# A decode block on one core: the last head's w_o rows four at a time, an empty pass skipped, the last V piece cut 10 + 6, and smaller edits to the layer norms and the gate product

## The chip, the cores and the metric

One Trainium2 chip, one core of it in use. The metric is the device time of one execution in microseconds (us), as a median over several executions. The engines named below are PE (TensorE: PE for its matmuls, PEld for its weight loads), DVE (VectorE), ACT (ScalarE), POOL (GpSimd) and SP (SyncE, which here only issues DMAs).

## The reference

One token (x is 1 x 512) goes through an attention block with a cached K and V, and then through a gated feed-forward block. All arrays are bfloat16.

```
h  = x + attention(layernorm(x))     # 32 query heads on 8 K/V heads; 65536 cached keys of 128 numbers each
     q = layernorm(x) @ wq           # 512 x 4096
     o = softmax(q k^T / sqrt(128)) v
     ... o @ wo                      # 4096 x 512
h2 = h + (sigmoid(n @ w_gate) * (n @ w_up)) @ w_down,   n = layernorm(h)   # 512 x 1792, 1792 x 512
```

K and V are 128 MB each; wq and wo 4 MB each; the three feed-forward weights 1.75 MB each. Each byte is read once, and the result is 1 KB.

## The kernel before

**Loads.** Every input but x goes through the one DMA queue of SP, in the order in which the program lists the loads (L332 to L361). K and V arrive in halves of a head (8 MB, `load`, L324) in a ring buffer in SBUF. A load waits for a mark that says that its place in the ring is free. For the last head the order in SP's queue is: the first half of V7 (L344); w_o in two pieces (L345 to L348, `WO`: the 28 rows per partition of heads 0 to 6, then the 4 of head 7), the first of which waits until PE is through with V6; the second half of V7 in two pieces (L349, `LAST`: 12 chunks of 512 KB, then 4); w_gate, w_up and w_down (L351 to L361), which wait until PE is through with the first half of V7. `WD_SPLIT` (L236) cuts w_down's 14 rows per partition into 8, 4 and 2.

**Attention.** DVE transposes K chunks (L517), PE computes scores of four blocks per head (`pe_scores`), ACT takes the exponentials, DVE transposes the probabilities, and PE multiplies them with V (`pv`, L591): a round is 8 matmuls, two chunks of V by four column groups of 32 of the PE array, the results in partitions 0, 32, 64 and 96 up. A half of V is 8 rounds: 6, a check, and 2. PE's program for all heads is one hand-written loop (`pe_flow`, L673) with a head as the outer step and four parts as the inner one. Register `w` counts the parts, `i` the heads, `m` and `k` the rounds. The V rounds of head h-1 run in parts 1 and 3 of head h. A ninth pass has no scores left and only does the V rounds of head 7: its parts 0 and 2 are empty, and PE goes through their branches and register instructions only. In its part 3, ahead of the second half of V7, stands section L (`project7`, L640): `regroup(0)` puts the outputs of heads 0 to 6 into 28 columns (L620 to L629), `rows` multiplies each of these columns (as 128 x 1 weights) with 512 columns of w_o, two matmuls to a pass of a loop, all into one row of PSUM (L645 to L663), DVE copies this row (L665), and `columns` turns it into four columns with float32 matmuls (L671). Section VL (L795) waits for the last piece of V7 ahead of the last two rounds.

**The tail.** `head_out` (L603) brings out head 7, `regroup(1)` and `project` (L631) add its 4 rows of w_o, which gives h as four columns of 128. `ln_stats` (L385) takes h, its square and their sums (four DVE instructions), and a matmul with ones adds over the partitions (L391). `hc` (L808) is h less its mean; the reciprocal deviation (`ln_rstd`, L394, with a power on POOL) is applied later, at the activation. 32 matmuls compute gate and up (L821), ACT takes the tanh that stands for the sigmoid (L828), DVE multiplies it with up (L831) and transposes the product (L834), 56 matmuls with one weight column each multiply it with w_down (L839, rows r = 0 to 13 by column groups g = 0 to 3), on top of h, which a matmul with `gsel` has put into the same four PSUM rows (L826). Two copies on DVE and two on ACT bring these rows into one row in SBUF (L845, L847), and one DMA from SP writes the 1 KB (L849). The program ends when that DMA has landed.

The layer norm of x at the start uses the same `ln_stats`; its result is needed by the query projection (L463), which also needs wq.

Of the kernel before, what the change touches and what calls it, by code (L numbers as in the profile page):

```python
# [6 lines left out]
bf16 = mybir.dt.bfloat16  # L7
# [8 lines left out]
NQ = 32  # L16
DH = 128
D = 512
# [197 lines left out]
def bass_sequential_preLN__gqa_block_cached__glu_gated_glu__decode_kernel(  # L216
# [19 lines left out]
    WD_SPLIT = [(0, 8), (8, 12), (12, 14)]  # L236
    FG = FF // 4

    with ExitStack() as es:
# [22 lines left out]
        yr = sb("yr", [1, 512], fp32)  # L262
        po_sb = sb("po_sb", [128, 512], bf16)
        one_f = sb("one_f", [1, 1], fp32)
        zcol = sb("zcol", [128, 1], bf16)
        XR = 16
# [27 lines left out]
        hhT = sb("hhT", [128, FG], bf16)  # L294
        y_sb = sb("y_sb", [1, D], bf16)
# [23 lines left out]
        LAST = [(16, 28), (28, 32)]  # L319
# [25 lines left out]
        for i, (j0, nj) in enumerate(WO):  # L345
            src = A_wo[j0 * DH:(j0 + nj) * DH, :].rearrange("(p r) n -> p (r n)", r=nj)
            dst = ktw[:, j0 * D:(j0 + nj) * D]
            dma("sp", lambda e, src=src, dst=dst: e.dma_start(dst, src), f"wo{i}", [f"PV{h - 1}.3"] if i == 0 else (), f"wo{i}")  # L348
        for i, cols in enumerate(LAST):  # L349
            load("V", h, 1, (), ("vb", "vl")[i], f"V{h}.1{('', 'b')[i]}", cols)  # L350
        for k, w in (("wg", B_w_gate), ("wu", B_w_up)):  # L351
            src = w.rearrange("(p k) n -> p (k n)", p=128)
            for i, (k0, k1) in enumerate(W_SPLIT[k]):
                at = W_AT[k]
                dma("sp", lambda e, at=at, w=src, a=k0 * FF, z=k1 * FF: e.dma_start(ring[:, at + a:at + z], w[:, a:z]),
                    f"{k}{i}", [f"PV{HKV - 1}.1"] if k == "wg" else (), f"{k}.{i}")
# [8 lines left out]
        for nm, t, v in (("onesf", onesf[:, :], 1.0), ("xz0", xz[:, :], 0.0), ("onef", one_f[:, :], 1.0), ("nhalf", nhalf[:, :], -0.5),  # L365
                         ("gs0", gsel[:, :], 0.0), ("zcol", zcol[:, :], 0.0), ("qh0", qh[:, :], 0.0), ("qz0", qz[:, :], 0.0),
                         ("PTz", PT_sb[:, 4 * 512:PT_ROW], 0.0), ("Wz", ktw[:, W0:KTW_ROW], 0.0)):
            op("pool", lambda e, t=t, v=v: e.memset(t, v), name=nm)
# [11 lines left out]
        op("dve", lambda e: e.tensor_reduce(bass.AP(tensor=gsel, offset=0, ap=[[128, 128], [32, 4]]),  # L380
                                            identf[:, :].rearrange("p (s j) -> p s j", s=4), AX.X, ALU.add), ["gs0", "identf"], "gsel")
# [3 lines left out]
        def ln_stats(i, fill, dep, bank, c0):  # L385

            op("dve", fill, [dep], f"hT.{i}")
            op("dve", lambda e: e.tensor_tensor(sq[:, :], hT[i][:, :], hT[i][:, :], ALU.mult), [f"hT.{i}"], f"sq.{i}")
            op("dve", lambda e: e.tensor_reduce(st[i][:, 0:1], hT[i][:, :], AX.X, ALU.add), (), f"sta.{i}")
            op("dve", lambda e: e.tensor_reduce(st[i][:, 1:2], sq[:, :], AX.X, ALU.add), [f"sq.{i}"], f"st.{i}")  # L390
            op("pe", lambda e: e.matmul(ps(bank, c0, c0 + 2), lhsT=onesf[:, :], rhs=st[i][:, :], start=True, stop=True),  # L391
               [f"st.{i}", f"sta.{i}", "onesf"], f"tot.{i}")
# [23 lines left out]
        ln_stats(0, lambda e: e.tensor_copy(hT[0][:, :], x_col[:, :]), "xcol", 0, 0)  # L416
# [54 lines left out]
        op("pe", project_q, ["zq", "xz", "wq", "identf", "lsel", "onef", "sel", "gsel", "row", "PTz", "qz0"], "q")  # L471
# [119 lines left out]
        def pv(h, r, rounds):  # L591
            P.part["pe"] = ("B", (h, r, rounds))
            name = f"PV{h}.{r}" + "a" * (rounds == 6)
# [46 lines left out]
        def project7():  # L640
            regroup(0)
            waits = ["O3.0", "wo0"]
            def rows(e):
                out = ps(YB, 0, D, 0, 1)
                e.matmul(out, lhsT=O3[:, 0:1], rhs=ktw[:, 0:D], start=True, stop=False, skip_group_check=True)  # L645
                ra, ro, rb, rp, left = (reg(e, i) for i in range(16, 21))
                n = NQ - GS
                e.reg_mov(ra, addr_of(ktw, D))
                e.reg_mov(ro, addr_of(O3, 1))
                e.reg_mov(left, n // 2 - 1)  # L650
                e.reg_alu(rb, ra, 2 * D, ALU.add)
                e.reg_alu(rp, ro, 2, ALU.add)
# [3 lines left out]
                for x in (ra, rb):  # L656
                    e.reg_alu(x, x, 4 * D, ALU.add)
                for x in (ro, rp):
                    e.reg_alu(x, x, 4, ALU.add)
# [3 lines left out]
                return e.matmul(out, lhsT=O3[:, n - 1:n], rhs=ktw[:, (n - 1) * D:n * D], start=False, stop=True, skip_group_check=True)  # L663
            op("pe", rows, waits, "yr")
            op("dve", lambda e: e.tensor_copy(yr[:, :], ps(YB, 0, D, 0, 1)), ["yr"], "yrs")  # L665

        def columns():

            for nt in range(4):
                lhsT = bass.AP(tensor=yr, offset=nt, ap=[[D, 1], [4, 128]])  # L670
                op("pe", lambda e, lhsT=lhsT, nt=nt: e.matmul(ps(YT, nt, nt + 1), lhsT=lhsT, rhs=one_f[0:1, 0:1], start=(nt == 0),  # L671
                                                              stop=False, skip_group_check=True), ["yrs"] if nt == 0 else ())
        def pe_flow(e, section):  # L673
# [7 lines left out]
            i, w, p, v, m, k, s = (R.setdefault(n, e.alloc_register(f"r_{n}")) for n in "iwpvmks")  # L681
# [8 lines left out]
            e.reg_mov(s, step[0])  # L690
            goto("head")
# [25 lines left out]
            away("br_eq", i, i_last, "rows_of_o", lambda: section("L"))  # L717
# [28 lines left out]
            e.reg_alu(w, w, -4, ALU.add)  # L746
            e.br_ne(w, w0 - 16, on_true="part", on_false="head_end")
            label("head_end")
            e.br_eq(i, i_last, on_true="after", on_false="more_heads")
            label("more_heads")  # L750
            section("X")
            e.reg_alu(i, i, -lag, ALU.add)
            nc.br("head", engines=here)
            for name, body, back, under in later:
                label(name, under)
                body()
                nc.br(back, engines=here)
            label("after", "head_end")
# [11 lines left out]
        for i in range(HKV + 1):  # L770
            loop, last = 0 < i < HKV, i == HKV
            for r in range(NR):
# [12 lines left out]
                if i and r == 3:  # L785
# [6 lines left out]
                    pv(i - 1, r, 6)  # L792
# [3 lines left out]
                    pv(i - 1, r, 2)  # L796
# [10 lines left out]
        ln_stats(1, lambda e: e.tensor_tensor(hT[1][:, :], ps(YT, 0, 4), x_col[:, :], ALU.add), "yT", STB, 0)  # L807
# [23 lines left out]
        op("dve", lambda e: e.tensor_tensor(hh[:, :].rearrange("p (r q) -> p r q", r=NF),  # L831
                                            ps(UB, 0, FG).rearrange("p (q r) -> p r q", r=NF),
                                            sg2[:, :].rearrange("p (q r) -> p r q", r=NF), ALU.mult), ["gu1", "sg2"], "hh")
        op("dve", lambda e: e.transpose(hhT[:, :], hh[:, :]), ["hh"], "hhT")  # L834
        for i, (r0, r1) in enumerate(WD_SPLIT):
            for r in range(r0, r1):
                for g in range(4):
                    last = r == NF - 1 and g == 3
                    op("pe", lambda e, r=r, g=g: e.matmul(  # L839
                        ps(YB, 0, 128, 32 * g, 32 * g + 1), lhsT=hhT[:, 32 * r:32 * r + 1], rhs=wd_v[:, r, g * 128:(g + 1) * 128],  # L840
                        start=False, stop=(r == NF - 1), tile_position=(0, 32 * g), skip_group_check=True),
                       ["hhT", f"wd{i}"] if r == r0 and g == 0 else (), "y" if last else None)
        for g in (0, 2, 1, 3):
            if g < 2:
                op("dve", lambda e, g=g: e.tensor_copy(y_sb[:, 128 * g:128 * g + 128], ps(YB, 0, 128, 32 * g, 32 * g + 1)), ["y"], f"ysb{g}")  # L845
            else:
                op("act", lambda e, g=g: e.activation(y_sb[:, 128 * g:128 * g + 128], ps(YB, 0, 128, 32 * g, 32 * g + 1), AF.Copy),  # L847
                   ["y"], f"ysb{g}")
        dma("sp", lambda e: e.dma_start(out[0], y_sb[:, :]), "out", [f"ysb{g}" for g in range(4)], "out")  # L849
        P.at_end = ("out",)  # L850
# [29 lines left out]
```

## Time and profile before

| | us |
|---|---|
| median of 3 runs | 658.86 (657.86 to 659.07) |
| the profiled execution | 658.92 |
| its span, first to last instruction | 657.6 |
| DMA: bytes read, mean rate over the span | 282.33 MB, 429 GB/s |
| PE busy | 403.7 (61%) |
| DVE busy | 350.7 (53%) |
| ACT busy | 42.9 (7%) |
| mean granted PE clock | 0.78 |

The profiled execution's own time is 1.3 us more than its span; the durations below come from this one execution. "Busy" counts work instructions only, not register, branch, semaphore and DMA-issuing ones. "Landing" of a DMA is counted from the start of its issue on the queue's engine. A row of the timeline gives the start, the time, the engine, the line, the operation, and in brackets the idle time before it with what ended it.

### The profile page before, as it was taken

To read this page: it belongs to the slowest core of one execution; us is meant where nothing else is said; L and a number is where in the kernel's file an instruction comes from. 1 tells how busy PE (TensorE), PEld (TensorE's weight loads), DVE (VectorE), ACT (ScalarE), POOL (GpSimd) and SP (SyncE) were. 2 spreads that over 40 slices of the span, in tenths; PEclk is the share of its full clock that TensorE was granted. 3 is DMA by queue.
4 is the path that set the end of the run, shared out by engine and by line. 5 is a ranking of instruction groups with operands and counts; after the bars stand their busy time and mean duration, and the time that the engine had idled before them with its cause. 6 is when DMAs were issued, how large, how long until landed. Compare 5 with 4: busy or idle time off the path is not lost. (4 is left out here: it accounts for less than half of the span.)

```text
span 657.6 us, 6197 instructions
## 1 busy us (share of the span) xinstructions
PE 403.7 (61%) x2316; PEld 68.8 (10%) x1548; DVE 350.7 (53%) x427; ACT 42.9 (7%) x114; POOL 3.6 (1%) x17
## 2 busy tenths in 40 slices
PE   2688672938547293764829476382946738285585
PEld 0100010110101010010100101010010101001132
DVE  3398853809266390936628183572908457193102
ACT  1100200020000200001000200002000020002001
POOL 1000000000000000000000000000000000000000
PEclk9889796867959587795958769595786959687677
DMA  9999999999999999999999999999999999999996
GB/s 399 431 440 452 442 419 415 446 446 442 431 403 446 446 446 435 395 446 446 446 435 399 442 446 446 442 407 427 446 446 442 419 415 446 446 442 431 419 410 291
DMA packets 6370, 282.33 MB, mean 429 GB/s; under 512 B 737, under 2 KB 738, under 8 KB 1250
## 3 DMA queue, kind: packets, MB, share of 16 engines
q1 hardware_dynamic: 6338, 282.33, 99.3%
q10 hardware_dynamic: 32, 0.00, 0.0%
HBM read 282.33 MB, written 0.00 MB: 429 GB/s over the span
## 5 line engine op out<-in xcount | busy, mean ns | idle before, releaser
L517 DVE STREAM_TRANSPOSE ktw<-ring 128x1024 f32<-128x1024 f32 x256 | 291.7, 1209 | 165.1 <-DMA ring<-in_A_k_cache_dram 165.1
L430 PE MATMUL PS<-ktw 128*128 128x512 bf16 x1024 | 277.8, 421 | 161.3 <-DVE ktw L517 157.5
L430 PE MATMUL PS<-ring,PT_sb 128*32 x1024 | 87.0, 430 | 51.4 <-issue 47.3
L430 PEld LDWEIGHTS PS<-ktw 128*128 x256 | 26.4, 103 | 401.3 <-issue 236.2
L604 ACT ACTIVATE po_sb<-PS,rl 128x512 bf16<-128x512 f32 x8 | 5.5, 687 | 525.0 <-PE PS L430 525.0
L430 PEld LDWEIGHTS PS<-ring,PT_sb 128*32 x1024 | 20.7, 116 | 115.2 <-issue 113.9
L552 DVE TENSOR_REDUCE gmj<-PS 1x4 f32<-1x128 f32 x8 | 2.2, 278 | 54.5 <-PE PS L550 54.5
L524 DVE TENSOR_REDUCE M_sb<-PS 128x1 f32<-128x512 f32 x32 | 19.9, 682 | 19.3 <-PE PS L430 19.3
L563 ACT ACTIVATE P_sb<-PS,negmax 128x512 bf16<-128x512 f32 x32 | 21.6, 686 | 0.3
L573 DVE STREAM_TRANSPOSE PT_sb<-P_sb 128x512 bf16<-128x512 bf16 x32 | 19.9, 675 | 1.7 <-ACT P_sb L563 1.7
L430 PE MATMUL PS<-ktw,xz 128*8 x32 | 8.8, 443 | 3.6 <-DMA ktw<-in_A_wq_dram 3.6
L620 DVE TENSOR_TENSOR Lw<-O,blk_of 128x896 bf16<-128x896 bf16 (+1 forms) x2 | 1.4, 682 | 13.0 <-ACT O L610 13.0
L550 PE MATMUL PS<-identf,gm 128*1 128x128 f32 x16 | 4.5, 380 | 5.5 <-issue 3.4
L629 DVE CAST O<-PS 128x28 bf16<-128x28 f32 (+1 forms) x2 | 0.3, 173 | 14.0 <-PE PS L626 14.0
L557 PE MATMUL PS<-one_f,gmrep 1*128 1x1 f32 x16 | 4.4, 344 | 5.0 <-DVE gmrep L554 5.0
L430 PE MATMUL PS<-ktw,O 128*1 x26 | 7.0, 433 | 0.0
L475 DVE STREAM_TRANSPOSE qt<-qh 32x512 bf16<-32x512 bf16 x1 | 0.7, 699 | 11.5 <-ACT qh L472 11.5
L563 ACT ACTIVATION_READ_ACCUMULATOR P_sb<-PS,negmax 128x1 f32 x32 | 6.5, 203 | 0.0
L607 PE MATMUL PS<-sel_bf,po_sb 128*128 128x4 bf16 x32 | 2.1, 171 | 6.3 <-ACT po_sb L604 6.3
L490 ACT ACTIVATE PS<-zcol 128x512 f32<-128x512 bf16 x8 | 5.0, 621 | 0.0
L559 ACT ACTIVATE negmax<-PS 128x1 f32<-128x1 f32 x8 | 1.4, 172 | 55.1 <-PE PS L557 55.1
L411 PE MATMUL PS<-xs,xpick 16*128 16x32 bf16 x1 | 0.2, 204 | 7.7 <-DMA xs<-in_A_x_dram 7.7
(88 smaller groups left out, 70.0 us busy)
## 6 DMA issues: line engine op xcount, KB each, us to landing
ring<-in_A_k_cache_dram SPq DMA_DIRECT2D x4, 4096.0 KB, 35.3
ring<-in_A_v_cache_dram SPq DMA_DIRECT2D x1, 6144.0 KB, 32.9
ktw<-in_A_wq_dram SPq DMA_DIRECT2D x1, 4096.0 KB, 12.5
ktw<-in_A_wo_dram SPq DMA_DIRECT2D x1, 3584.0 KB, 18.0
ring<-in_A_v_cache_dram SPq DMA_DIRECT2D x1, 2048.0 KB, 37.3
ring<-in_B_w_gate_dram SPq DMA_DIRECT2D x1, 1792.0 KB, 23.3
ring<-in_B_w_up_dram SPq DMA_DIRECT2D x1, 1344.0 KB, 26.0
ring<-in_B_w_down_dram SPq DMA_DIRECT2D x1, 1024.0 KB, 28.7
```

The source lines that it names most:

```text
L430: return e.add_instruction(mybir.InstMatmult(name=nc.get_next_instruction_name(), engine=mybir.EngineType.PE, ins=[rhs, lhsT], outs=[e.low ...
L490: op("act", lambda e: e.activation(ps(PO, 0, 512), bass.AP(tensor=zcol, offset=0, ap=[[1, 128], [0, 512]]), AF.Copy), ["zcol"] if h == 0 e ...
L517: op("dve", lambda e, d=dst, sr=src: e.transpose(d, sr), deps, f"T{b}.{c}", to="T")
L524: op("dve", lambda e, u=u: e.tensor_reduce(M_sb[:, u % 4:u % 4 + 1], ps(u % NS, 0, 512), AX.X, ALU.max), [f"S{b}.{NC - NR + k}"], f"mx{u}" ...
L550: op("pe", lambda e: e.matmul(ps(MISC, 0, 128, 0, 1), lhsT=gm[:, :], rhs=identf[:, :], start=True, stop=True), [f"gm{h}"], f"gmT{h}", to="Q")
L552: op("dve", lambda e: e.tensor_reduce(gmj[:, :], ps(MISC, 0, 128, 0, 1).rearrange("p (i a c) -> p a i c", a=4, c=NC), AX.XY, ALU.max), [f" ...
L557: op("pe", lambda e: e.matmul(ps(MISC, 128, 129), lhsT=gmrep[0:1, :], rhs=one_f[0:1, 0:1], start=True, stop=True), [f"gmrep{h}"], f"neg{h}")
L559: op("act", lambda e: e.activation(negmax[:, k:k + 1], ps(MISC, 128, 129), AF.Copy, scale=-att_scale), [f"neg{h}"], f"negmax{h}")
L563: op("act", lambda e, b=b: e.activation(P_sb[:, (b % 4) * 512:(b % 4 + 1) * 512], ps(b % NS, 0, 512), AF.Exp, bias=negmax[:, k:k + 1], sca ...
L573: op("dve", lambda e, b=b: e.transpose(PT_sb[:, (b % 4) * 512:(b % 4 + 1) * 512], P_sb[:, (b % 4) * 512:(b % 4 + 1) * 512]), [f"E{b}"], f" ...
L604: op("act", lambda e: e.activation(po_sb[:, :], ps(PO, 0, 512), AF.Copy, scale=rl[:, :]), [f"PV{h}.{NR - 1}", f"rl{h}"], f"po{h}", to="po")
L607: op("pe", lambda e, t=t: e.matmul(ps(OX, 0, 4), lhsT=po_sb[:, t * 128:(t + 1) * 128], rhs=sel_bf[:, 8 * t:8 * t + 8:2], start=(t == 0), s ...
```

## The change

- `LAST` cuts the second half of V7 into 10 + 6 chunks, and PE does 5 rounds, the check, and 3. The second piece of w_o (4 rows, 512 KB) is issued behind the V pieces and not ahead of them.
- The ninth pass enters the loop at part 1 and steps by 8 to part 3, so that its empty parts 0 and 2 are not gone through; register `d` holds the step. The loop's way out now stands behind section O of that pass.
- `rows` does four w_o rows to a pass of its loop, one in each column group, into PSUM rows 0, 32, 64, 96 of a bank that ACT clears early (`zy`). So all 128 partitions are copied (L665), and `columns` adds the four by weights of 128 x 128 and a selecting column.
- `ln_stats` takes two DVE instructions that multiply or add two operands and sum the result.
- The gate product and its transpose come in two parts (rows 0 to 6, 7 to 13). `WD_SPLIT` is 9, 4, 1.
- The result's even column groups use 32 weight columns, of which the last is the real one, so that groups 0 and 1 end in the neighbouring partitions 31 and 32, and 2 and 3 in 95 and 96. One copy on DVE and one on ACT, of 33 partitions each, and two DMAs of 2 x 256 B, one issued by SP and one by ACT, take the place of four copies and one DMA.

```diff
-    WD_SPLIT = [(0, 8), (8, 12), (12, 14)]
+    WD_SPLIT = [(0, 9), (9, 13), (13, 14)]
-        LAST = [(16, 28), (28, 32)]
+        LAST = [(16, 26), (26, 32)]
...
+        load_wo(0, [f"PV{h - 1}.3"])
         for i, cols in enumerate(LAST):
             load("V", h, 1, (), ("vb", "vl")[i], f"V{h}.1{('', 'b')[i]}", cols)
+        load_wo(1, ())
...
-            op("dve", fill, [dep], f"hT.{i}")
-            op("dve", lambda e: e.tensor_tensor(sq[:, :], hT[i][:, :], hT[i][:, :], ALU.mult), [f"hT.{i}"], f"sq.{i}")
-            op("dve", lambda e: e.tensor_reduce(st[i][:, 0:1], hT[i][:, :], AX.X, ALU.add), (), f"sta.{i}")
-            op("dve", lambda e: e.tensor_reduce(st[i][:, 1:2], sq[:, :], AX.X, ALU.add), [f"sq.{i}"], f"st.{i}")
+            op("dve", lambda e: e.tensor_tensor_reduce(hT[i][:, :], parts[0], parts[1], 1.0, 0.0, ALU.add, ALU.add, st[i][:, 0:1]), [dep], f"hT.{i}")
+            op("dve", lambda e: e.tensor_tensor_reduce(sq[:, :], hT[i][:, :], hT[i][:, :], 1.0, 0.0, ALU.mult, ALU.add, st[i][:, 1:2]),
+               [f"hT.{i}"], f"st.{i}")
...
+        op("act", lambda e: e.activation(ps(5, 0, 512), bass.AP(tensor=zcol, offset=0, ap=[[1, 128], [0, 512]]), AF.Copy), (), "zy")
...
-                for x, y in ((ra, ro), (rb, rp)):
-                    mm_at(e, out, at_reg(O3, y, [[NQ, 128], [1, 1]]), at_reg(ktw, x, [[KTW_ROW, 128], [1, D]]), False, 32)
+                for g in range(4):
+                    mm_at(e, ps(YB, 0, D, 32 * g, 32 * g + 1), at_reg(O3, ys_[g], [[NQ, 128], [1, 1]]),
+                          at_reg(ktw, xs_[g], [[KTW_ROW, 128], [1, D]]), False, 32, 32 * g)
...
-            op("dve", lambda e: e.tensor_copy(yr[:, :], ps(YB, 0, D, 0, 1)), ["yr"], "yrs")
+            op("dve", lambda e: e.tensor_copy(yr[:, :], ps(YB, 0, D)), ["yr"], "yrs")
-                lhsT = bass.AP(tensor=yr, offset=nt, ap=[[D, 1], [4, 128]])
+                lhsT = bass.AP(tensor=yr, offset=nt, ap=[[D, 128], [4, 128]])
...
-            e.reg_alu(w, w, -4, ALU.add)
+            e.reg_alu(w, w, d, ALU.add)
             e.br_ne(w, w0 - 16, on_true="part", on_false="head_end")
             label("head_end")
-            e.br_eq(i, i_last, on_true="after", on_false="more_heads")
-            label("more_heads")
             section("X")
             e.reg_alu(i, i, -lag, ALU.add)
-            nc.br("head", engines=here)
+            e.br_ne(i, i_last, on_true="head", on_false="last_head")
+            label("last_head")
+            e.reg_mov(w, w0 - 4)
+            e.reg_mov(p, p0)
+            e.reg_mov(d, -8)
+            nc.br("values", engines=here)
...
-                    pv(i - 1, r, 6)
+                    pv(i - 1, r, 5 if last else 6)
...
-                    pv(i - 1, r, 2)
+                    pv(i - 1, r, 3 if last else 2)
...
+        HH = ((0, 7), (7, NF))
+        for i, (r0, r1) in enumerate(HH):
+            op("dve", lambda e, r0=r0, r1=r1: e.tensor_tensor(
+                hh[:, 32 * r0:32 * r1].rearrange("p (r q) -> p r q", q=32),
+                ps(UB, 0, FG).rearrange("p (q r) -> p r q", r=NF)[:, r0:r1, :],
+                sg2[:, :].rearrange("p (q r) -> p r q", r=NF)[:, r0:r1, :], ALU.mult), ["gu1", "sg2"], f"hh{i}")
+            op("dve", lambda e, r0=r0, r1=r1: e.transpose(hhT[:, 32 + 32 * r0:32 + 32 * r1], hh[:, 32 * r0:32 * r1]), [f"hh{i}"], f"hhT{i}")
...
+                    m, c = (1, 32 * r + 32) if g % 2 else (32, 32 * r + 1)
...
+        op("dve", lambda e: e.tensor_copy(y_sb[0:33, :], ps(YB, 0, 128, 0, 33)), ["y"], "ysb0")
+        op("act", lambda e: e.activation(y_sb[64:97, :], ps(YB, 0, 128, 64, 97), AF.Copy), ["y"], "ysb1")
+        for i, eng in enumerate(("sp", "act")):
+            dst = out[0][:, 256 * i:256 * i + 256].rearrange("o (s j) -> (o s) j", s=2)
+            dma(eng, lambda e, i=i, dst=dst: e.dma_start(dst, y_sb[64 * i + 31:64 * i + 33, :]), f"out{i}", [f"ysb{i}"], f"out{i}")
+        P.at_end = ("out0", "out1")
```

Left out: a zeroed column `zf` for the first layer norm, a zeroed start of `hhT`, `gsel` with its ones at columns 31, 32, 95 and 96, a matmul with zeros that closes `rows`, and the wait of the query projection for `zy`.

More of the change, by code (lines that the diff above doesn't have):

```diff
@@ L293, in bass_sequential_preLN__gqa_block_cached__glu_gated_glu__decode_kernel @@
         hh = sb("hh", [128, FG], bf16)
-        hhT = sb("hhT", [128, FG], bf16)
-        y_sb = sb("y_sb", [1, D], bf16)
+        hhT = sb("hhT", [128, 32 + FG], bf16)
+        y_sb = sb("y_sb", [128, 128], bf16)
         W0 = NKT * CH
@@ L592, in pv @@
             P.part["pe"] = ("B", (h, r, rounds))
-            name = f"PV{h}.{r}" + "a" * (rounds == 6)
+            name = f"PV{h}.{r}" + "a" * (rounds > 3)
             for k in range(2):
@@ L643, in rows @@
             def rows(e):
[L644 to L646 removed]
                 n = NQ - GS
[L648 to L652, printed above, removed]
[L653 to L659 removed]
+                xs_, ys_, left = [reg(e, 16 + g) for g in range(4)], [reg(e, 20 + g) for g in range(4)], reg(e, 24)
+                e.reg_mov(xs_[0], addr_of(ktw))
+                e.reg_mov(ys_[0], addr_of(O3))
+                e.reg_mov(left, n // 4)
+                for g in range(1, 4):
+                    e.reg_alu(xs_[g], xs_[0], 2 * D * g, ALU.add)
+                    e.reg_alu(ys_[g], ys_[0], 2 * g, ALU.add)
+                goto("rows")
+                for g in range(4):
+                    mm_at(e, ps(YB, 0, D, 32 * g, 32 * g + 1), at_reg(O3, ys_[g], [[NQ, 128], [1, 1]]),
+                          at_reg(ktw, xs_[g], [[KTW_ROW, 128], [1, D]]), False, 32, 32 * g)
+                for g in range(4):
+                    e.reg_alu(xs_[g], xs_[g], 2 * 4 * D, ALU.add)
+                    e.reg_alu(ys_[g], ys_[g], 2 * 4, ALU.add)
                 e.reg_alu(left, left, -1, ALU.add)
@@ L756, in pe_flow @@
                 body()
-                nc.br(back, engines=here)
-            label("after", "head_end")
+                if name == "outs":
+                    e.br_ne(i, i_last, on_true=back, on_false="after")
+                else:
+                    nc.br(back, engines=here)
+            label("after", "outs")
         def dve_flow(e, section):
@@ L838, in bass_sequential_preLN__gqa_block_cached__glu_gated_glu__decode_kernel @@
                     last = r == NF - 1 and g == 3
-                    op("pe", lambda e, r=r, g=g: e.matmul(
-                        ps(YB, 0, 128, 32 * g, 32 * g + 1), lhsT=hhT[:, 32 * r:32 * r + 1], rhs=wd_v[:, r, g * 128:(g + 1) * 128],
+                    m, c = (1, 32 * r + 32) if g % 2 else (32, 32 * r + 1)
+                    op("pe", lambda e, r=r, g=g, m=m, c=c: e.matmul(
+                        ps(YB, 0, 128, 32 * g, 32 * g + m), lhsT=hhT[:, c:c + m], rhs=wd_v[:, r, g * 128:(g + 1) * 128],
                         start=False, stop=(r == NF - 1), tile_position=(0, 32 * g), skip_group_check=True),
[L842 to L850, printed above, removed]
+                       ((["hhTz", f"wd{i}"] if r == r0 else []) + [f"hhT{j}" for j, (h0, _) in enumerate(HH) if r == h0]) if g == 0 else (), "y" if last else None)
+        op("dve", lambda e: e.tensor_copy(y_sb[0:33, :], ps(YB, 0, 128, 0, 33)), ["y"], "ysb0")
[4 more added lines that the diff above has]
+        P.at_end = ("out0", "out1")
         P.emit()
```

42 lines of the change are left out of this document (23 added, 19 removed).

## The prediction

> **What bounds the kernel now.** I read the page's load lines first: is the stream of loads ever interrupted?
>
> ```profile
> span 657.6 us, 6197 instructions
> ...
> DMA  9999999999999999999999999999999999999996
> ```
>
> All 40 slices but the last are full, so nothing in the middle of the kernel can shorten it: every byte has to come in, and the time is the end of the stream plus what follows it. So the question is where the stream ends. The start of each issue is in the views by line and in the timeline, the time to landing in the DMA view:
>
> ```profile
> L348 SPq DMA_DIRECT2D ktw<-in_A_wo_dram x2: 328/380/433, 602.0 to 602.3; - x2
> 602.82 0.91 SPq L330 DMA_DIRECT2D ring<-in_A_v_cache_dram  x2
> L355 SPq DMA_DIRECT2D ring<-in_B_w_up_dram x2: 432/434/435, 622.0 to 622.5; - x2
> L360 SPq DMA_DIRECT2D ring<-in_B_w_down_dram x3: 432/432/432, 623.0 to 623.9; - x3
> ```
>
> ```profile
> ktw<-in_A_wo_dram SPq DMA_DIRECT2D x1, 3584.0 KB, 18.0
> ktw<-in_A_wo_dram SPq DMA_DIRECT2D x1, 512.0 KB, 18.9
> ring<-in_A_v_cache_dram SPq DMA_DIRECT2D x1, 6144.0 KB, 32.9
> ring<-in_A_v_cache_dram SPq DMA_DIRECT2D x1, 2048.0 KB, 37.3
> ring<-in_B_w_up_dram SPq DMA_DIRECT2D x1, 448.0 KB, 26.7
> ring<-in_B_w_down_dram SPq DMA_DIRECT2D x1, 1024.0 KB, 28.7
> ring<-in_B_w_down_dram SPq DMA_DIRECT2D x1, 512.0 KB, 29.5
> ring<-in_B_w_down_dram SPq DMA_DIRECT2D x1, 256.0 KB, 29.6
> ```
>
> Start plus time (of a merged pair, the second starts half its time later: V's at 603.3): w_o lands at 620.0 and 621.2, the last V half at 635.7 (12 chunks) and 640.6, the last of w_up at 649.2, w_down at 651.7, 652.9 and **653.5**. The 6144 KB took 635.7 - 621.2 = 14.5 us, 424 KB per us; 37.3 - 18.9 us and the others give the same pace, so these loads run one behind the other.
>
> The span goes on for 4.1 us after the last landing. What fills it is in the chain of waits (start, us, what):
>
> ```profile
> 635.83 0.46 issue
> 636.29 5.58 PE PS L430 x42
> 641.87 1.33 issue
> 643.21 0.63 PE PS L430 x8
> ...
> 644.91 0.70 ACT po_sb L604
> ...
> 647.76 0.17 DVE hT L807
> ...
> 648.37 0.60 PE PS L391 x2
> ...
> 648.99 0.17 DVE hc L808
> ...
> 649.21 3.19 PE PS L821 x18
> ...
> 652.42 0.93 DVE hh L831
> ...
> 653.37 0.66 DVE hhT L834
> ...
> 654.07 1.69 PE PS L839 x56
> ...
> 656.09 0.28 DVE y_sb L845
> ```
>
> It begins when the 12 chunks of V land (635.7), and from there never waits for a load again: the other V chunks (640.6) and all weights are in before they are asked for, and the last matmuls start 0.5 us after the last landing, because of `hhT`. So **today compute from V7 on sets the end, with the stream of loads only half a microsecond behind.** A shorter chain can win that half microsecond; what more there is lies in the matmuls that stand behind the last landing, and in the output.
>
> **The change: loads.** The bytes stay. With w_o's 512 KB behind V and 10 chunks (5120 KB), the first V piece lands at 620.0 + 5120/424 = 632.1, the second (3072 KB) at 639.4, w_o's rest at 640.6 as V's end did. w_gate, w_up and w_down keep their places. w_down as 9 + 4 + 1: from 649.2, the first 1024 KB took 2.5, so 1152 KB 2.8: 652.0; then as before 1.2 (512 KB): 653.2; then 128 KB, half of 0.6: 653.5. The last piece comes in 1 KB runs, shorter than any weight run of before; the pace of 2 KB runs (256 KB in 0.6) is that of the long ones, so I count nothing; twice the price would be 0.3 us, which the range takes in. SP issues as many loads as before, and V's are no longer behind one of w_o's.
>
> **PE up to V7.** These rows carry it:
>
> ```profile
> 624.06 0.45 PEld L626 LDWEIGHTS PS<-row_of,Lw 128*128 128x128 bf16 x7 [3.24 <-issue]
> 625.26 6.97 PE L430 MATMUL PS<-ktw,O 128*1 x26
> 632.49 0.68 DVE L665 COPY yr<-PS 1x512 f32<-1x512 f32 x1 [7.66 <-PE PS L663]
> 633.22 2.02 PE L671 MATMUL PS<-one_f,yr 1*128 1x1 f32 x8 [0.77 <-DVE yr L665]
> 636.28 0.16 PEld L430 LDWEIGHTS PS<-ring,PT_sb 128*32 x8 [1.13 <-issue]
> 641.23 0.16 PEld L430 LDWEIGHTS PS<-ring,PT_sb 128*32 x8 [0.81 <-issue]
> ```
>
> Between V7's first half and the weights of 624.06 PE idles through part 2's empty pass and part 3's branches; halving that saves about 1.2. Of the 28 w_o rows 26 take 6.97, so all take 7.5. Four at a time are what a V round does twice; a round takes (641.23 - 636.28)/5 = 0.99, so seven passes take 3.5: 4 us less. The copy (L665) and `columns` (L671) now work on 128 partitions, which isn't in the trace: from below as long as before (0.7 + 2.0), from above twice that. I take the first, since the columns are as many. So PE is ready for V7 near 630.0 instead of 635.2 (633.22 + 2.02). **All that is worth nothing by itself**: it is covered by the wait for V, which ends at 632.1; at twice the price PE is ready at 632.7, which costs 0.6 of the 1.8 us that it then waits for the next piece. But without it V would start 3 us late: old `columns` ended only 0.5 before the old landing.
>
> V resumes at 632.1 + 0.5 = 632.6; 5 rounds end near 637.6, and **a new wait** of 1.8 us comes, for the 6 chunks at 639.4. Behind it on PE stand the last rounds and everything after; the feed-forward weights do not wait for it. It resumes after 0.5 (as after 635.83) to 1.3 us (the gap at 641.87); I take 0.6: 640.0. Three rounds: 2.0 to the last one's start, and 0.63 to 1.0 for it by the clock: 642.7 to 643.0, against 644.9. So the chain is about 2 us earlier at po_sb.
>
> **The tail's small edits.**
>
> ```profile
> L430 PE MATMUL PS<-ktw,xz 128*8 x32 | 8.8, 443 | 3.6 <-DMA ktw<-in_A_wq_dram 3.6
> L388 DVE TENSOR_TENSOR sq<-hT 128x4 f32<-128x4 f32 x1 | 0.2, 163 | 0.0
> L563 ACT ACTIVATION_READ_ACCUMULATOR P_sb<-PS,negmax 128x1 f32 x4 | 0.8, 203 | 0.0
> L839 PEld LDWEIGHTS PS<-ring,hhT 128*1 128x1 bf16 x56 | 1.4, 120 | 1.3 <-DVE hhT L834 1.3
> L810 DVE TENSOR_TENSOR hz<-sel_f,hT 128x128 f32<-128x128 f32 x1 | 0.3, 281 | 0.0
> ```
>
> Layer norm: from 647.76 to the matmul at 648.37 is 0.61. Two dependent instructions of 0.2 (163 ns plus a gap) make 0.45: 0.15 less. An instruction with a sum isn't in the trace; if the sum is read out separately as on ACT (203 ns each), it is 0.25 more. I take -0.15, being nearest to L388. For x it hardly matters: the query matmuls wait for wq (the first row). Extra clears (POOL, 0.1 each; ACT 0.6) lie in the first 5 us, where both idle later.
>
> From po_sb to hc were 648.99 - 644.91 = 4.1, from hc to the end of gate and up 3.4. So hc comes at 646.6 to 647.2 (the upper with short matmuls at half clock), the others end at 650.0 to 650.6 (w_up's last piece, 649.2, is in before its turn). Gate product: two halves of 0.54 (of 0.92, 0.16 fixed as at L388 and the rest by columns) and two transposes of 0.34 with gaps: 1.9 instead of 1.6. The first half is ready near 651.3, the second near 652.3. The w_down rows take 1.69/14 = 0.12 each: rows 0 to 8 from 652.0 (landing) to 653.1, rows 9 to 12 from 653.25 to 653.75, the last row, whose load is then in, to **653.9**, against 655.76. 32 weight columns cost no more than one: 8 of V's loads take 0.16 together, 56 of these 1.4. **So the loads are last again**, and the chain has a spare: `hhT`'s second half may come at 653.05 (0.85 before 653.9), 0.75 later than I count.
>
> Output: one copy per engine instead of two: 0.3 less; 33 partitions for one I count as free (281 ns for 128 x 128 at L810). The copies end at 654.2.
>
> ```profile
> 656.44 0.32 SPq L849 DMA_DIRECT2D out_dram<-y_sb  x1
> xs<-in_A_x_dram ACTq DMA_DIRECT2D x1, 1.0 KB, 6.9
> ```
>
> From issue to the end of the span are 657.6 - 656.44 = 1.16. Two DMAs with 256 B rows, one from ACT, aren't in the trace. Nearest row below: that 1.16; above: 6.9, ACT's own 1 KB load, but beside the first loads. At the end the queues are empty, so I take 1.16. Issue 654.27, end 655.43: **2.17 us less**, 1.9 by the matmuls and 0.3 by the copies. 658.92 - 2.17 = 656.75; the median lies 0.06 lower: **656.7**.
>
> A rule against it stands in the Trainium skill, DMA: Bandwidth & Descriptors, Specifications: under 512 B a transfer becomes a read-modify-write. By its section Latency and other measured facts a round trip to HBM is at least 0.8 us; I estimate 657.5 from that. No row here shows it: the 64 B pieces of x were read, not written.
>
> **Rivals.**
> 1. *The chain stays last.* For it: it is last now, and gains a wait. All upper bounds together (1.3 after the wait, half clock, 0.25 more for the sums) put `hhT` at 653.55 and the end 0.5 behind my sum: 657.2; half a microsecond more in an unforeseen stall gives 657.7. Against: 0.75 us of spare.
> 2. *Short output rows cost an extra trip to memory.* Bounded by one more 1.16: up to 657.9. Against: it is a matter of 1 KB.
> 3. *Slower: ACT's output queue.* If its first row takes the 6.9 us that ACT's queue took at the start, the end is 654.27 + 6.9 = 661.2, 662.5 in all. It decides from 1.16 + 2.17 = 3.3 us on. Against: those 6.9 us ran beside full DMA engines.
> 4. *It doesn't do what it says:* the last w_down row or the last V wait is no earlier because loads shift by as much. Then only the copies are won: 658.6.
>
> **Numbers.** Forecast 0.74 (its own range 656.0 to 657.3, with the scatter of the three runs), rival 1 0.11, rival 2 0.05, rival 3 0.04, rival 4 0.06. A measurement tells about 0.2% (1.3 us) from no change: faster is the forecast and most of rivals 1 and 2 below 657.5 (0.83), the same the rest of them and rival 4 (0.13), slower rival 3 (0.04). The range 656.0 to 657.8 leaves out rivals 3 and 4 and the ends of 1 and 2.
>
> **What would show it.** In the new profile: V's pieces at 632.1 and 639.4, w_down at 652.0, 653.2, 653.5; PE idle ahead of VL, waiting for a DMA; `hhT` ready ahead of 653; the w_down matmuls broken into pieces that wait for loads and end 0.4 after the last landing; one copy on each engine; some 1.2 us from the issue of the output to the end. It is wrong if the last w_down matmuls still start with `hhT`, or if the last landing moves from 653.5.

## The result and the profile after

| | before | after |
|---|---|---|
| median, us | 658.76 (657.86 to 659.07, 8 runs) | 656.80 (656.46 to 657.16, 8 runs) |
| profiled execution, its span | 658.92, 657.6 | 656.78, 655.5 |
| last landing of a load | 653.5 | 653.3 |
| last w_down matmul ends | 655.8 | 653.8 |
| output's issue on SP | 656.44 | 654.16 |

The ratio is 0.9971, 95% interval 0.9961 to 0.9982: about 2 us less. From the last landing to the end of the span there were 4.1 us and are 2.2; that is the change. The other 0.2 of the span is the whole stream of loads, which lies that much earlier in this execution; its last landing lies between 653.1 and 654.0 in the profiles below, with the order of the loads or without.

The loads, first from the timeline (start, time, engine, line), the view of line L365, and the DMA view (KB, us from issue to landing):

```profile
602.23 0.91 SPq L331 DMA_DIRECT2D ring<-in_A_v_cache_dram  x2
```

```profile
L365 SPq DMA_DIRECT2D ring<-in_B_w_down_dram x3: 432/432/432, 622.2 to 623.2; - x3
```

```profile
ring<-in_A_v_cache_dram SPq DMA_DIRECT2D x1, 5120.0 KB, 29.7
ring<-in_A_v_cache_dram SPq DMA_DIRECT2D x1, 3072.0 KB, 36.5
...
ring<-in_B_w_down_dram SPq DMA_DIRECT2D x1, 1152.0 KB, 29.5
...
ring<-in_B_w_down_dram SPq DMA_DIRECT2D x1, 512.0 KB, 30.3
...
ring<-in_B_w_down_dram SPq DMA_DIRECT2D x1, 128.0 KB, 30.1
```

Start plus time: V lands at 631.9 and 639.2 (forecast 632.1, 639.4), w_down at 651.7, 653.0 and 653.3 (forecast 652.0, 653.2, 653.5). The end of the chain of waits of the changed kernel now holds a load, which it didn't before:

```profile
622.71 30.31 DMA ring<-in_B_w_down_dram
653.02 0.04 issue
653.07 0.76 PE PS L861 x16
653.82 0.02 issue
653.85 0.28 DVE y_sb L865
```

And its timeline from V on; the bracket says what ended the idle time before:

```profile
628.20 2.03 PE L676 MATMUL PS<-sel_f,yr 128*128 128x1 f32 x8 [0.80 <-DVE yr L670]
...
632.43 5.04 PE L435 MATMUL PS<-ring,PT_sb 128*32 x40 [2.21 <-PEq L171]
...
639.81 0.63 PE L435 MATMUL PS<-ring,PT_sb 128*32 x8 [2.34 <-DMA ring<-in_A_v_cache_dram]
...
642.90 0.69 ACT L610 ACTIVATE po_sb<-PS,rl 128x512 bf16<-128x512 f32 x1 [34.82 <-PE PS L435]
...
650.74 0.41 DVE L855 STREAM_TRANSPOSE hhT<-hh 128x224 bf16<-128x224 bf16 x1
...
651.59 0.41 DVE L855 STREAM_TRANSPOSE hhT<-hh 128x224 bf16<-128x224 bf16 x1
651.83 0.88 PEld L861 LDWEIGHTS PS<-ring,hhT 128*32 128x32 bf16 x36 [1.28 <-DMA ring<-in_B_w_down_dram]
651.83 1.96 PE L861 MATMUL PS<-ring,hhT 128*32 128x128 bf16 x56 [0.98 <-DMA ring<-in_B_w_down_dram]
653.07 0.46 PEld L861 LDWEIGHTS PS<-ring,hhT 128*32 128x32 bf16 x20 [0.36 <-DMA ring<-in_B_w_down_dram]
653.85 0.27 ACT L866 ACTIVATE y_sb<-PS 33x128 bf16<-33x128 f32 x1 [4.53 <-PE PS L861]
653.85 0.28 DVE L865 CAST y_sb<-PS 33x128 bf16<-33x128 f32 x1 [1.84 <-PE PS L861]
654.15 0.50 ACTq L869 DMA_DIRECT2D out_dram<-y_sb  x1
654.16 0.33 SPq L869 DMA_DIRECT2D out_dram<-y_sb  x1
```

PE is through with w_o at 630.2 and waits for V twice, 2.2 and 2.3 us. (The first of the two is put down to `PEq`, PE's own sequencer, which holds the wait; V lands at 631.9, 0.5 ahead of the round.) The first part of `hhT` is there (651.15) ahead of the first load of w_down (651.7), the second (652.0) ahead of the next (653.0), and the last matmuls start with a load.

### The profile page after: what moved, and what is told of

The parts are those of the page before. It is cut to its first block, busy times and chain, and to the rows that moved or that the text cites. A ratio compares the mean times of both kernels' runs of the same rounds, so it can differ in the third digit from the quotient of the medians.

```text
span 655.5 us, 6177 instructions
## 1 busy us (share of the span) xinstructions
PE 400.4 (61%) x2317; PEld 66.9 (10%) x1549; DVE 350.4 (53%) x428; ACT 43.1 (7%) x114; POOL 3.7 (1%) x19
## 4 chain that ended last, share of the span: by engine, by line
DMA 66%; DVE 29%; PE 3%; issue 1%; SPq 0%; PEldq 0%
DMA ring<-in_A_k_cache_dram 58%; DVE ktw L523 29%; DMA ring<-in_B_w_down_dram 5%; DMA ring<-in_A_v_cache_dram 4%; PE PS L435 3%; SPq L360 0%; PE PS L861 0%; SPq L365 0%; SPq L331 0%; DVE y_sb L865 0%; PEldq L171 0%
## 5 line engine op out<-in xcount | busy, mean ns | idle before, releaser
L584 PE MATMUL PS<-L_sb,lsel 128*128 128x4 f32 x16 | 2.5, 229 | 3.8 <-DVE PT_sb L579 3.8
```

The source lines that it names most:

```text
L584: op("pe", lambda e: e.matmul(ps(MISC, 132, 136), lhsT=lsel[:, :], rhs=L_sb[:, :], start=True, stop=True), [f"PT{NR * h + NR - 1}"], f"l{h ...
```

## The experiments

Theory at first: loads set the end as soon as the chain from V on is early enough; for that the order of the loads and less work on PE (the shorter w_o rows above all) are needed together, and the tail's edits bring little. Of this, "the shorter rows above all" fell with E7, and E11 and E12 say what stands in its place. Rivals stand in the expectations. Each kernel was run beside the kernel before; its ratio to that is given.

**E1: the loads in the old order, V as 12 + 4, all else changed.**

```diff
-        LAST = [(16, 26), (26, 32)]
+        LAST = [(16, 28), (28, 32)]
         load_wo(0, [f"PV{h - 1}.3"])
+        load_wo(1, ())
...
-        load_wo(1, ())
-                    pv(i - 1, r, 5 if last else 6)
+                    pv(i - 1, r, 6)
```

> The changed kernel with the loads in their old order (w_o whole ahead of V's second half) and V as 12 + 4 chunks, 6 and 2 rounds; all other edits stay. Theory (the earlier chain from V on is what brings the last matmuls up to the last landing): V's 12 chunks land at 635.6 again, PE stands ready from 630.2, po_sb is at 644.8 as before, the second half of hhT at 654.0, and the last w_down matmul ends near 654.8 instead of 653.83: 657.8 (657.4 to 658.2). Rival (the edits of the tail bring the gain, the order of the loads is hidden): 656.8.

Measured: 658.05, ratio 0.9988 (0.9979 to 0.9997): 1.2 us of the gain are gone, 0.7 are left to the other edits. The timeline of this kernel's one profiled execution (of 657.24, span 655.9: one of the shorter ones, the median span is 656.7):

```profile
635.88 1.05 PE L435 MATMUL PS<-ring,PT_sb 128*32 x8 [5.79 <-PEq L171]
```

```profile
653.19 0.41 DVE L853 STREAM_TRANSPOSE hhT<-hh 128x224 bf16<-128x224 bf16 x1
653.66 0.40 PEld L859 LDWEIGHTS PS<-ring,hhT 128*32 128x32 bf16 x28 [0.37 <-DVE hhT L853]
653.66 0.57 PE L859 MATMUL PS<-ring,hhT 128*32 128x128 bf16 x28 [0.20 <-DVE hhT L853]
```

PE waits 5.8 us for V; at the end `hhT` releases the matmuls again, and not a load. The rival (the tail's edits bring the whole gain) falls.

**E2: the kernel before with the order of the loads and 10 + 6 alone.**

```diff
-        LAST = [(16, 28), (28, 32)]
+        LAST = [(16, 26), (26, 32)]
+        load_wo(0, [f"PV{h - 1}.3"])
         for i, cols in enumerate(LAST):
             load("V", h, 1, (), ("vb", "vl")[i], f"V{h}.1{('', 'b')[i]}", cols)
+        load_wo(1, ())
+                    pv(i - 1, r, 5 if last else 6)
+                    pv(i - 1, r, 3 if last else 2)
```

> The kernel before with the new order of the loads and V as 10 + 6 chunks, 5 and 3 rounds, alone. Theory (the w_o rows must be shorter for the earlier V to be used): V lands at 632.1, but PE is in the w_o rows and columns until 635.2 and starts V's rounds near 635.8 instead of 636.3; the end is at most 0.4 us earlier: 658.4 (658.2 to 658.8). Rival (the order of the loads does it alone): 657 to 657.5.

Measured: 658.5, ratio 0.9992 (0.9983 to 1.0001). Its timeline:

```profile
625.02 8.25 PE L434 MATMUL PS<-ktw,O 128*1 x26
...
634.25 2.02 PE L675 MATMUL PS<-one_f,yr 1*128 1x1 f32 x8 [0.77 <-DVE yr L669]
636.21 0.58 PEld L434 LDWEIGHTS PS<-ring,PT_sb 128*32 x16
```

V had landed at 631.9, but PE is with w_o until 636.2: the earlier load is not used. (The 28 rows took 8.8 us here, from 624.6 to 633.5, more than the 7.5 I had counted from the profile of before, so V's rounds start no earlier than there. The windows view has PE's granted clock at 0.50 up to 630 here, and at 1.00 from 628 on in the profile of before.)

The median hides that the executions fall into two groups: four of the eleven have spans of 655.7 to 656.3, and seven of 657.0 to 657.7; none of the 33 of the kernel before is under 656.6, and with both halves (E4 below) they are 655.3 to 656.1. The profiled one is of the longer group. So in some executions the order alone brings the gain or most of it. The 1.3 us by which the rows differ with the clock are as much as what E11 below takes off PE, which may explain it; but no execution of the shorter group was profiled, and this is not shown.

**E3: the kernel before with the w_o rows four at a time and the skipped parts alone.**

```diff
+                for g in range(4):
+                    mm_at(e, ps(YB, 0, D, 32 * g, 32 * g + 1), at_reg(O3, ys_[g], [[NQ, 128], [1, 1]]),
+                          at_reg(ktw, xs_[g], [[KTW_ROW, 128], [1, D]]), False, 32, 32 * g)
...
+            e.reg_alu(w, w, d, ALU.add)
...
+            e.reg_mov(w, w0 - 4)
+            e.reg_mov(p, p0)
+            e.reg_mov(d, -8)
+            nc.br("values", engines=here)
```

> The kernel before with the w_o rows four at a time and the empty parts of the last pass skipped, alone; loads, layer norm, gate product, output as before. Theory (5 us less of PE work is all covered by the wait for V): PE is ready at 630.2 and waits for V until 635.7; everything behind is as before: 658.8 (658.5 to 659.0). Rival (PE's work up to V is part of what sets the end): 1 us or more less, below 657.8.

Measured: 658.62, ratio 1.0002 (0.9993 to 1.0011): nothing. Its timeline:

```profile
636.16 1.05 PE L435 MATMUL PS<-ring,PT_sb 128*32 x8 [5.80 <-PEq L171]
```

Five microseconds less work on PE have become 5.8 us of waiting for V.

**E4: both, with the tail as before** (layer norm of four instructions, gate product in one part, w_down 8 + 4 + 2, four copies, one DMA). Against the changed kernel:

```diff
-    WD_SPLIT = [(0, 9), (9, 13), (13, 14)]
+    WD_SPLIT = [(0, 8), (8, 12), (12, 14)]
-        HH = ((0, 7), (7, NF))
+        HH = ((0, NF),)
...
+            op("dve", lambda e: e.tensor_reduce(st[i][:, 0:1], hT[i][:, :], AX.X, ALU.add), (), f"sta.{i}")
+            op("dve", lambda e: e.tensor_reduce(st[i][:, 1:2], sq[:, :], AX.X, ALU.add), [f"sq.{i}"], f"st.{i}")
...
+        dma("sp", lambda e: e.dma_start(out[0], y_sb[:, :]), "out", [f"ysb{g}" for g in range(4)], "out")
```

> The kernel before with the order of the loads, 10 + 6, the rows four at a time and the skipped parts, but layer norm, gate product in one part, w_down 8 + 4 + 2 and the output as before. Theory (with the chain early, the loads set the end and the edits of the tail are hidden but for the output): hhT is whole near 652.0, the last w_down piece (2 rows) lands at 653.4, the last matmul ends near 653.75, four copies take 0.6, one output DMA 1.16: span 655.6, time 656.9 (656.7 to 657.3). Rival (the tail's edits bring half of the gain): 657.8.

Measured: 657.17, ratio 0.9973 (0.9964 to 0.9982), not to be told from the changed kernel's 0.9971; the span is 655.5 in both. Its timeline:

```profile
651.21 0.65 DVE L855 STREAM_TRANSPOSE hhT<-hh 128x448 bf16<-128x448 bf16 x1
...
652.70 0.21 PEld L861 LDWEIGHTS PS<-ring,hhT 128*1 128x1 bf16 x16 [0.26 <-DMA ring<-in_B_w_down_dram]
653.29 0.10 PEld L861 LDWEIGHTS PS<-ring,hhT 128*1 128x1 bf16 x8 [0.39 <-DMA ring<-in_B_w_down_dram]
```

Alone the first was 0.3 less (its interval reaches 1.0001) and the second nothing, together they are 1.6 less: in the median neither half works without the other, and with both the last matmuls of this execution wait for loads, so that the tail's edits are hidden.

**E5: the changed kernel without w_down's loads** (they are left out, and the matmuls read what V left).

```diff
-        for i, (r0, r1) in enumerate(WD_SPLIT):
-            at = AT["wd"] * CH
-            dma("sp", ...
-                       ((["hhTz", f"wd{i}"] if r == r0 else [])
+                       ((["hhTz"] if r == r0 else [])
```

> The changed kernel without the three loads of w_down (it leaves them out: the last matmuls read what V left in the ring). The stream of loads ends with w_up, at 649.0 instead of 653.3. Theory (the loads are last, and the chain is some 0.8 us behind them): the last matmuls now start with the first half of hhT at 651.15, the second half comes at 652.0, they end at 652.6 to 652.9 by the clock instead of 653.83: about 1 us less, 655.8 (655.4 to 656.1). Rival (the chain has much spare behind the loads): the 4.3 us of the loads are won, 652.5. Rival (the chain is still last): no change, 656.8.

Measured: 655.94, ratio 0.9953 (0.9939 to 0.9967): 0.9 less than the changed kernel, though 4.3 us of loads are gone. Its timeline:

```profile
651.07 0.67 PEld L855 LDWEIGHTS PS<-ring,hhT 128*32 128x32 bf16 x28 [0.66 <-DVE hhT L849]
...
651.94 0.67 PEld L855 LDWEIGHTS PS<-ring,hhT 128*32 128x32 bf16 x28 [0.20 <-DVE hhT L849]
652.93 0.27 ACT L860 ACTIVATE y_sb<-PS 33x128 bf16<-33x128 f32 x1 [3.75 <-PE PS L855]
```

This is the chain by itself: it ends 0.9 before the loads let it (652.93 against 653.85). Of that 0.1 is no spare, since this execution is that much ahead at `po_sb` already (642.78 against 642.90); 0.8 are left, where the prediction had put 0.75.

**E6: the changed kernel with the old output** (one weight column, four copies, one DMA of 1 KB).

```diff
-                    m, c = (1, 32 * r + 32) if g % 2 else (32, 32 * r + 1)
+                    m, c = 1, 32 * r + 32
...
+        dma("sp", lambda e: e.dma_start(out[0], y_sb[:, :]), "out", [f"ysb{g}" for g in range(4)], "out")
```

> The changed kernel with the output as before: one weight column per matmul, four copies, one DMA of 1 KB from SP. Prediction's step: 0.3 us later by the copies and the same 1.16 from issue to end. What the trace of the changed kernel shows beside it: issue to end took 1.34 there, so the net is 0.1 to 0.15: copies 0.59, issue near 654.5, span 655.6, time 656.9. Rival (short rows of 256 B cost a trip to memory more): the old output would be faster, 656.3 or less.

Measured: 656.88, ratio 0.9966 (0.9953 to 0.9978): no difference in time. In its timeline (span 655.7) the copies take 0.3 longer and the rest is shorter:

```profile
653.84 0.59 DVE L867 CAST y_sb<-PS 1x128 bf16<-1x128 f32 x2 [1.85 <-PE PS L861]
654.50 0.32 SPq L871 DMA_DIRECT2D out_dram<-y_sb  x1
```

From the issue to the end are 655.7 - 654.50 = 1.2, in the changed kernel 655.5 - 654.16 = 1.34.

**E7: the changed kernel with the w_o rows two at a time, as before.**

```diff
+                for x, y in ((ra, ro), (rb, rp)):
+                    mm_at(e, out, at_reg(O3, y, [[NQ, 128], [1, 1]]), at_reg(ktw, x, [[KTW_ROW, 128], [1, D]]), False, 32)
```

> The changed kernel with the w_o rows two at a time into one PSUM row, as before, skipped parts and load order kept. Theory (PE waits 1.9 us for V's 10 chunks and 2.3 for the last 6, and the chain has 0.8 us of spare after that): PE is ready 4 us later, at 634.2, V's rounds start at 634.7 instead of 632.4 and reach the check at 639.9, after the landing of 639.2; they go on at 640.3 instead of 639.8, the spare takes the 0.5: 656.8 (656.6 to 657.1). Rival (the rows are on the path now): 658 or more.

Measured: 657.0, ratio 0.9971 (0.9961 to 0.9981). Its timeline:

```profile
634.91 4.13 PE L435 MATMUL PS<-ring,PT_sb 128*32 x40
...
639.98 0.42 PE L435 MATMUL PS<-ring,PT_sb 128*32 x4 [0.95 <-DMA ring<-in_A_v_cache_dram]
```

PE comes to V 2.5 us later and reaches the check as V's last chunks land (639.2); it goes on 0.2 after the changed kernel. So the rows are not on the path, as expected; but then they aren't needed either, and what E2 lacks on PE up to V should be the skip of the empty parts. E11 and E12 try that, on the kernel before with the new order of the loads: E11 adds the skip and leaves the rows, E12 adds the rows and leaves the empty parts.

**E11: order of the loads and skip. E12: order of the loads and rows.** Both have the tail as before. E11 is E4 with the diff of E7; E12 is E4 with

```diff
-            e.reg_alu(w, w, d, ALU.add)
+            e.reg_alu(w, w, -4, ALU.add)
-            e.br_ne(i, i_last, on_true="head", on_false="last_head")
+            nc.br("head", engines=here)
```

> The kernel before with the order of the loads, 10 + 6 and the skipped parts; w_o rows two at a time and the tail as before. Rows needed (the prediction's reading, that the shorter rows are what the earlier V needs): PE comes to V some 4 us late, little is won, 658.0 to 658.5. Skip enough (the run with the old rows and the rest of the change reached V's check just as its last chunks landed): V's rounds start near 634.9, go on at 640.0, po_sb 642.7 to 643.0, hhT whole near 652, the last w_down matmul ends near 653.7: 657.2, as with rows and skip together.

> The kernel before with the order of the loads, 10 + 6 and the w_o rows four at a time, without the skipped parts; the tail as before. If the early V needs PE to be early by any means: PE is ready at 631.5, before V (631.9), and the time is that of both together: 657.2. If the skip does something of its own: 658 or more.

Measured: E11 657.0, ratio 0.9971 (0.9961 to 0.9981); E12 657.38, ratio 0.9979 (0.9970 to 0.9988). The timeline of E11 and, in the second fence, of E12:

```profile
634.38 4.06 PE L435 MATMUL PS<-ring,PT_sb 128*32 x40
...
642.72 0.69 ACT L610 ACTIVATE po_sb<-PS,rl 128x512 bf16<-128x512 f32 x1 [34.85 <-PE PS L435]
...
651.90 1.66 PE L862 MATMUL PS<-ring,hhT 128*1 128x128 bf16 x56 [1.07 <-DVE hhT L856]
653.62 0.59 DVE L868 CAST y_sb<-PS 1x128 bf16<-1x128 f32 x2 [1.86 <-PE PS L862]
```

```profile
632.58 5.01 PE L435 MATMUL PS<-ring,PT_sb 128*32 x40 [0.98 <-PEq L171]
...
643.05 0.69 ACT L610 ACTIVATE po_sb<-PS,rl 128x512 bf16<-128x512 f32 x1 [34.80 <-PE PS L435]
...
652.32 1.66 PE L854 MATMUL PS<-ring,hhT 128*1 128x128 bf16 x56 [1.07 <-DVE hhT L848]
654.03 0.59 DVE L860 CAST y_sb<-PS 1x128 bf16<-1x128 f32 x2 [1.86 <-PE PS L854]
```

The rows leave PE free from 631.6 on, and V's rounds start with the landing; with the skip alone they start some 2 us later, and po_sb comes no later for it (the whole stream lies 0.3 later in E12), since in between stands the wait for V's last chunks (639.0 and 639.3). **With the order of the loads, 1.3 us less on PE ahead of V are enough for the gain that was measured**: the skip alone does it (PE idles 1.94 us and not 3.24 ahead of `regroup(0)`), the rows alone do it too, and both together bring nothing more that can be measured. Whether less than 1.3 would do was not tried.

Two things go with this. E12's higher median comes from outside its span: five of its eleven executions took 2.1 to 2.7 us more than their span, the others 1.3 to 1.6; the median spans are 655.5 (E11), 655.7 (E12), 655.5 (E4) and 655.5 (changed kernel). And with the old tail the spare is gone: in both timelines the 56 matmuls of w_down start with `hhT` and run in one piece, and the loads land 0.2 to 0.4 us before their rows' turn. There the chain sets the end, only just. Both ran these matmuls at a granted clock of 0.50 (1.66 us); E4's profile, with the same tail, had 1.00 there, and the loads set the end. So what the tail's edits buy is spare: in the changed kernel's profile the clock was 0.50 from 652 to 654 too, and the loads were last.

**E8: w_down as 9 + 3 + 1 + 1.**

```diff
-    WD_SPLIT = [(0, 9), (9, 13), (13, 14)]
+    WD_SPLIT = [(0, 9), (9, 12), (12, 13), (13, 14)]
```

> The changed kernel with w_down in four loads of 9, 3, 1 and 1 rows instead of 9, 4 and 1. Theory (the last matmuls end 0.5 after the last landing because the five last rows run as one row of matmuls from the landing of the 4-row load, 653.0, on): with row 12's load apart the last row alone is left at 653.3, and the matmuls end near 653.65 instead of 653.83: 0.2 less, 656.6. Rival (one more load of 1 KB runs costs as much as it brings): 656.8 or more.

Measured: 656.89, ratio 0.997 (0.9959 to 0.9981): no gain, the rival's 656.8 or more. Its last load was issued at 623.8 and landed 29.8 later, at 653.6. (SP was held by one of the four issues for 8.09 us, by the others for 0.43 each; nothing stands behind them in its queue but the output.) Its timeline:

```profile
653.57 0.11 PEld L861 LDWEIGHTS PS<-ring,hhT 128*32 128x32 bf16 x4 [0.23 <-DMA ring<-in_B_w_down_dram]
653.93 0.27 ACT L866 ACTIVATE y_sb<-PS 33x128 bf16<-33x128 f32 x1 [4.69 <-PE PS L861]
```

The last row alone is left, and it needs 0.36 from its first weight load to the copy; with 9 + 4 + 1 it was 0.5 from the last landing. The 0.15 are below what the runs can tell.

**E9 and E10: the output's DMAs.** What are the 0.18 us by which two DMAs of 2 x 256 B are slower than one of 1 KB? E9 issues both from SP; E10 writes the old single row by two DMAs of 512 B, from SP and ACT.

```diff
-        for i, eng in enumerate(("sp", "act")):
+        for i, eng in enumerate(("sp", "sp")):          (E9)
+            dma(eng, lambda e, i=i: e.dma_start(out[0][:, 256 * i:256 * i + 256], y_sb[:, 256 * i:256 * i + 256]), ...   (E10)
```

> The changed kernel with both output DMAs issued by SP. The changed kernel's output took 1.34 from SP's issue to the end, against 1.16 for one DMA of 1 KB; open is what the 0.18 is. If it is ACT's queue (its issue takes 0.50 against 0.33), the second issue of SP comes 0.33 later and the end 1.16 after that: 1.5 from the first issue. If it is the DMA of two rows of 256 B, each takes 1.34 and the end is at 1.67 from the first issue.

> The changed kernel with the old four copies into one row, and this row written by two DMAs of 512 B, one from SP and one from ACT. If the 0.18 comes from two rows in one DMA, issue to end is 1.16 as for one DMA of 1 KB. If it comes from the second DMA or from ACT's queue, it is 1.34 again.

One execution each; E9's span is 656.3, E10's 656.0 (the loads lay later in both):

```profile
654.79 0.64 SPq L869 DMA_DIRECT2D out_dram<-y_sb  x2
```

```profile
654.65 0.32 SPq L872 DMA_DIRECT2D out_dram<-y_sb  x1
```

E9: 656.3 - 654.79 = 1.5, as for two DMAs like the old one, issued 0.37 apart. E10: 656.0 - 654.65 = 1.35, though its rows are single. So rows of 256 B cost nothing here; the 0.18 come with a second DMA from the other queue at the same time. The traces also hold when each output DMA landed. Of E9's two, each landed 1.1 us after its issue (1.12 and 1.10), as a single one of 1 KB did (1.13 in the kernel before and in E6). With two at once, ACT's landed after 1.11 (the changed kernel and E10) and SP's after 1.27 and 1.28, though the packets of both moved within 0.1 us of each other. So it isn't ACT's queue that is slower: it is SP's DMA that lands later when ACT's is under way beside it. Why is not shown.

## Why the prediction was right, point by point

- **"The question is where the stream ends":** right. The last landing stayed at 653.1 to 653.6 in all these profiles but E9's (654.0, with the whole stream later) and E5's, which leaves it out, and the gain lies behind it.
- **"All that is worth nothing by itself", "But without it V would start 3 us late":** the first is shown by E3. The second is right in E2's profile (636.2, with V there at 631.9) and was put down to too large an edit: of the 5 us that PE wins 1.3 are enough, because the wait for V's last chunks, which the prediction names itself, takes up whatever is late ahead of it. The skip, counted there as 1.2 and covered, is enough alone (E11).
- **The new wait:** as forecast. PE was ready at 630.2 (forecast 630.0; the rows took 3.8, where 3.5 were counted, copy and `columns` as long as before, as taken). Five rounds ended at 637.5, and V's last chunks landed 1.7 later, at 639.2 (forecast 1.8); resuming cost 0.6, as taken: 639.8. The 2.34 of the timeline are both together. po_sb came at 642.90 (forecast 642.7 to 643.0).
- **Layer norm:** 646.12 - 645.69 = 0.43 from `hT` to the matmul instead of 0.61, forecast 0.45. The sum is read out by an instruction of its own, as on ACT, but it takes 0.08 and not 0.2:

```profile
645.69 0.16 DVE L392 CUSTOM_DVE_ANT_0 hT<-PS,x_col 128x4 f32<-128x4 f32 x1 [0.80 <-PE PS L642]
645.78 0.08 DVE L392 DVE_READ_ACCUMULATOR2_ANT st<- 128x1 f32 x1
```

- **hhT:** 651.15 and 652.0, forecast 651.3 and 652.3. E4 shows that the two parts are hidden: whole at 651.86, it was early too.
- **Last matmuls:** they end 0.5 behind the last landing, forecast 0.4. The load ahead of them sets this end, not the last: 20 matmuls run in one piece from 653.07, and the last row's load is long in when its turn comes. **Mis-sized** by 0.1; E8, which cuts this piece, won nothing that can be measured.
- **Output:** the copies brought the 0.3. "I take 1.16" was **mis-sized**: 1.34. Net 0.15 instead of 0.3. The rule of the Trainium skill weighed there (DMA: Bandwidth & Descriptors, Specifications: under 512 B a read-modify-write) does not show in these times: E9's DMAs of 256 B rows landed after 1.12 and 1.10 us, the one of 1 KB after 1.13.
- **Sum:** the tail fell by 4.1 - 2.2 = 1.9 where I had 2.17; the stream, 0.2 earlier in the one profiled execution, made up for it there, and the medians are 1.96 apart. That the forecast was met to 0.1 is in part luck; the mechanism is what the runs bear out. None of the rivals came: the chain has 0.8 of spare (E5), and ACT's output DMA landed after 1.11 us, not 6.9.

## What to carry to other kernels

In a kernel whose loads run without a gap, read the end of the loads and ask what stands between the last landing and the end; only that, and a chain that is later than the loads, can be won. Two edits that each measure as nothing may be two halves of one: an earlier load needs an engine that is ready for it, and an engine that is ready sooner needs the load; try pairs, and the smallest pair, for a wait behind both may forgive most of the lateness. Read the single executions too: a median between two groups, as in E2, hides that one half alone sometimes brings most of the gain. Once the loads are last, further edits of the chain that runs beside them measure as nothing, however right they are.

## What the runs showed of the hardware

**The PE clock's phase moves the end when the chain is last.** I had counted w_down's matmuls at half clock. These two rows of the windows view (PE busy, then PEld, DVE, ACT, POOL, the granted clock, DMA share, GB/s), of the kernel before and of E3, show the same 56 matmuls with a clock of 0.50 and 1.00:

```profile
654.00:655.00 1.00, 0.93 (x40) 0.94 (x44) 0.01 (x1) 0.00 (x0) 0.00 (x0) 0.50 0.00 0
```

```profile
654.00:655.00 1.00, 0.89 (x56) 0.70 (x55) 0.06 (x1) 0.06 (x1) 0.00 (x0) 1.00 0.00 0
```

They took 1.66 and 0.95 us. That goes with E3's profiled span of 656.8, while its median time of 658.62 is that of the kernel before (658.78). The spans of the kernels with the chain last scatter more (E1: 655.7 to 657.5 in 11 runs; E2: 655.7 to 657.7 in 11; E3: 656.6 to 657.9 in 11) than those with the loads last (the changed kernel: 655.1 to 655.8 in 8; E6: 655.3 to 655.7 in 6; E7: 655.4 to 655.8 in 9); that the clock is the reason was not tried by itself.

**A round of V's matmuls comes no sooner at the full clock.** Rounds start 0.97 to 1.03 us apart whether the eight matmuls take 0.63 (E1 from 640 on, granted clock 1.00) or 1.05 (the changed kernel from 632.43 on, clock 0.50). At the full clock PE idles 0.34 to 0.40 between two rounds and waits for nothing that the profile shows; the loop's register and branch instructions stand there, but that they fill this time was not tried.
